# Rows of three chunks turned by transposing transfers on the SyncE queue in place of TensorE transposes, with later loads issued behind the normalising

## The chip, the cores and the metric

The kernel runs on one core of one Trainium2 chip. A core has five engines that run side by side, each through its own list of instructions in a fixed order: TensorE (PE in the profile; PEld is its weight load), VectorE (DVE), ScalarE (ACT), GpSimd (POOL) and SyncE (SP), which here does nothing but issue DMA transfers. Engines wait for one another by semaphores. On-chip memory has 128 partitions; matrix results land in a separate memory, PSUM. The metric is the device time of one execution in microseconds (us): 178.88 us as the median of three runs of the kernel before (178.66 to 179.46).

## The reference

The input is a matrix of 2048 rows (tokens) by 512 columns. Each row is normalised, and two branches work on the normalised rows: a two-dimensional Fourier filter and a gated feed-forward layer of width 1792. The result is the sum of the input and both branches, in bf16.

```python
def _A_ref(x, w_r, w_i):                    # x: 1 x 2048 x 512
    X = rfft2(x.astype(float32))            # 2048 x 257
    X = X * (w_r + 1j * w_i)
    return irfft2(X, s=(S, D)).astype(bfloat16)

def _B_ref(x, w_gate, w_up, w_down):        # 512 x 1792, 512 x 1792, 1792 x 512
    g = einsum("bsd,df->bsf", x, w_gate)
    u = einsum("bsd,df->bsf", x, w_up)
    return einsum("bsf,fd->bsd", gelu(g) * u, w_down)

x = A_x
xn = _layernorm(x, axis=-1)
return x + _A_ref(xn, A_w_r, A_w_i) + _B_ref(xn, B_w_gate, B_w_up, B_w_down)
```

## The kernel before

**Tiling.** The 2048 rows are 16 row tiles of 128 rows (s = 0 to 15), in four chunks of four tiles (b = 0 to 3). `x_sb` holds the rows, `specB` among other things the normalised rows (`xn`, L500: eight buffers, tile s uses buffer s mod 8), and `xnT` the normalised rows turned, that is, with the 512 columns on the partitions in four blocks of 128. Everything that TensorE does with the rows reads `xnT`.

**A row tile's way.** `stats` (L503) takes mean and variance on DVE, `root_pool` (L513) the reciprocal root on POOL for four tiles at once, `norm` (L519) writes the normalised tile on DVE. `turn` (L524) turns one or two tiles: four PE transposes of 128 by 128 per tile into a PSUM buffer, and one DVE copy from there to `xnT` (L539). Tiles 0 to 3 are turned one by one, tiles 4 to 15 in pairs.

**The feed-forward branch.** `gated` (L648) multiplies a chunk with one block of 128 columns of `w_gate` and of `w_up` (PE, L657), ACT brings both results from PSUM to `gg` and `uu` (four buffers each, L662 and L663), DVE multiplies them into `hT` (L664). `down` (L692) multiplies `hT` with `w_down` (`wd`). The list `filler` (L722 on) gives the order of this work: chunk 0, then chunk 1 with the down products of chunk 0 among it, and so on; the down products of chunk 3 end the kernel.

**The spectral branch.** `fold` (L545) adds and subtracts parts of a turned chunk on DVE and multiplies it on PE with `smallc` (L570). After four chunks DVE does butterflies, PE multiplies with `tokf` (L782), DVE multiplies with the filter `filt` (L450, between L795 and L843), PE multiplies with `toki` (L859, L860), DVE does butterflies again, PE multiplies with `smallc` (L924), and the result is added to `x_sb`. `filt` holds the filter twice: as it is, and mirrored. The mirrored half is made by six transfers from the inputs to a scratch tensor in device memory, `w_mirror` (L616 to L618), and loaded from there. POOL computes two small tensors, `edge`, one from the real and one from the imaginary part of the whole filter (L792).

**What sets the order.** All instructions are operations of a planner (`_Sched`). Each has a planned cost, a key or a due time, and its predecessors follow from what it reads and writes. The planner steps through time, and of the operations that an engine can start next it takes the one with the lowest priority number: the time at which it becomes ready plus its key, or its due time. The order of each engine is then fixed in the program; at run time an instruction waits for its semaphores and everything behind it on its engine waits too. For a transfer the planner counts a cost on the issuing queue and then a common pipe for all bytes; the costs are written in the code, 0.41 us for a plain transfer, and 3.5, 2.5 and 2.0 us for the three mirror transfers of each part.

**Transfers on SP.** In order: rows and weights of the feed-forward branch, `smallc`, the rows of chunks 2 and 3, then `wd`, `tokf`, `toki` (L608 to L610), the six mirror transfers, the direct and mirrored loads of `filt`, and a few small ones. All of these have no predecessor but the first row tile's load (the list `gate`, whose entries every later transfer on SP takes as predecessors, L445), the mirrored loads excepted, which follow the mirror transfers. The result's stores come last.

Of the kernel before, what the change touches and what calls it, by code (L numbers as in the profile page):

```python
# [16 lines left out]
NFC = 14  # L17
# [111 lines left out]
class _Sched:  # L129
# [11 lines left out]
    def op(self, eng, cost, fn, reads=(), writes=(), tiles=(), key=0.0, after=(), dma=0, lag=0.0, due=None):  # L141
        o = _Op()
        o.eng, o.fn, o.cost, o.key, o.dma, o.lag, o.due = eng, fn, cost, key, dma, lag, due
        o.reads, o.writes, o.tiles = reads, writes, [(t, False) for t in tiles]
        o.extra = [a for a in after if a is not None]
        o.seq = len(self.ops)
        o.end = None
        o.pos = None
        self.ops.append(o)
        return o  # L150
# [182 lines left out]
def bass_parallel_sum__spectral_gfnet__glu_gated_geglu__prompt_kernel(  # L333
# [19 lines left out]
    wdv = B_w_down.rearrange("(fc p) d -> p fc d", p=P)  # L353

    sch = _Sched()
    op = sch.op

    with ExitStack() as es:
        def sb(name, shape, dt=BF16, cell=0):
            n = int(np.prod(shape))  # L360
            t = es.enter_context(nc.sbuf_tensor(name, [P, n], dt))
            return view(t, name, 0, shape, cell)
# [14 lines left out]
        xnT = sb("xnT", [4, 4, 4, P])  # L377
        wg = sb("wg", [4, FF])
        wu = sb("wu", [4, FF])
        wd = sb("wd", [NFC, D])  # L380
# [61 lines left out]
        gate = []  # L442

        def dma(q, dst, src, nbytes, wr=None, rd=None, key=0.0, after=(), cost=0.41, lag=0.0):
            after = tuple(after) + tuple(gate if q == "sp" else ())  # L445
            return op(q, cost, lambda e: e.dma_start(dst() if callable(dst) else dst.ap, src() if callable(src) else src.ap),  # L446
                      reads=rd if rd is not None else (), writes=wr if wr is not None else (), dma=nbytes, key=key, after=after, lag=lag)
# [7 lines left out]
        def load(q, dst, src, nbytes, **kw):  # L455
            return dma(q, dst, lambda: src, nbytes, wr=(dst,), **kw)

        def blk(s):
            return (s - 1) % 16
# [4 lines left out]
        k = iter(np.arange(0.0, 1.0, 0.001))  # L464
        first_row = None
        for s in range(4):
            o = load("sp", x[:, s], xb[:, blk(s), :], 131072, key=next(k))
# [32 lines left out]
        def xn(s):  # L500
            return RB(8192 + 512 * (s % 8), [4, P])

        def stats(s, key, due=None, after=()):  # L503
            op("dve", 0.61, lambda e: e.bn_stats(bst[:, s].ap, xs(s).ap), reads=(xs(s),), writes=(bst[:, s],), key=key, due=due, after=after)  # L504
            op("dve", 0.11, lambda e: e.bn_aggr(bag[:, s].ap, bst[:, s].ap), reads=(bst[:, s],), writes=(bag[:, s],), key=key, due=due)
# [7 lines left out]
        def root_pool(s0, n, key):  # L513
            sl = slice(s0, s0 + n)
            v, y, h = vv[:, sl], rs[:, sl], half[:, sl]
            op("pool", 0.2 + 0.03 * n, lambda e: e.tensor_scalar(v.ap, bag.ap[:, sl, 1], LN_EPS, None, ADD), reads=(bag[:, sl],), writes=(v,), key=key)
            op("pool", 0.5 + 0.14 * n, lambda e: e.tensor_tensor(y.ap, v.ap, h.ap, ALU.pow), reads=(v, h), writes=(y,), key=key)

        def norm(s, key, due=None):  # L519
            o, i = xn(s).rs([512]), xs(s)  # L520
            op("dve", 0.34, lambda e: e.tensor_scalar(o.ap, i.ap, bag.ap[:, s, 0:1], rs.ap[:, s:s + 1], SUB, MUL),
               reads=(i, bag[:, s], rs[:, s:s + 1]), writes=(o,), key=key, due=due)

        def turn(s0, n, key):  # L524
            b, sl = s0 // 4, s0 % 4
            t = _T("sp")

            def bank():
                return ps_sp_bf[:, t.slot * 2048:t.slot * 2048 + 512 * n]

            def f(e):
                ins = None
                for i in range(4 * n):
                    ins = e.transpose(bank()[:, i * P:(i + 1) * P], xn(s0 + i // 4).ap[:, i % 4], ident.ap)  # L534
                return ins

            o = xnT[:, b, sl:sl + n].rs([512 * n])
            op("pe", 4 * n * 0.056, f, reads=tuple(xn(s0 + i) for i in range(n)) + (ident,), tiles=(t,), key=-40, lag=0.1)
            op("dve", 0.08 + n * 0.26, lambda e: e.tensor_copy(o.ap, bank()), writes=(o,), tiles=(t,), key=key)  # L539


        Y = R1(0, [8, 2, D])
        H = R3(0, [8, 2, D])
        X = R1(0, [8, 2, D])
        def fold(b):  # L545
            par = b % 2
            a = RB(2048 * par, [4, 2, P])
            f = RB(4096 + 2048 * par, [4, 4, P])
            z = R3(2048 * par, [2, 2, 512])
            xt = xnT[:, b]  # L550
            kk = 2.0
            tt(a, xt[:, :, 0:2], xt[:, :, 2:4], ADD, 1024, kk)
            tt(f[:, :, 0], a[:, :, 0], a[:, :, 1], ADD, 512, kk)
            tt(f[:, :, 1], a[:, :, 0], a[:, :, 1], SUB, 512, kk)
            tt(f[:, :, 2:4], xt[:, :, 0:2], xt[:, :, 2:4], SUB, 1024, kk)
            fv = f.rs([2, 2, 4, P])
            zv = z.rs([2, 2, 4, P])
            tt(zv[:, :, 0], fv[:, :, 1], fv[:, :, 0, :, ::-1], ADD, 1024, kk)
            tt(zv[:, :, 1], fv[:, :, 1], fv[:, :, 0, :, ::-1], SUB, 1024, kk)
            for j in range(2):  # L560
                t = _T("sp")

                def f_c(e, z=z, j=j, t=t):
                    ins = None
                    for o in range(2):
                        bank = spb(t, o).rearrange("p (s r i) -> p s r i", s=2, r=4)
                        for cc in range(4):
                            to = bank[:, :, 2 * cc] if cc < 2 else bank[:, :, 1::2]
                            mat = Tf.ap[:, cc] if cc < 2 else Tf.ap[:, 2 * cc - 2:2 * cc]
                            ins = e.matmul(to, z.ap[:, j, o, cc * P:(cc + 1) * P], mat, start=(cc == 0), stop=(cc == 3))  # L570
                    return ins

                op("pe", 4 * 0.057 + 4 * 0.11, f_c, reads=(z[:, j], Tf), tiles=(t,), key=kk, lag=0.1)
                jp = 2 * b + j
                yv = Y[:, jp].rs([4, 64, 4])
                op("act", c_act(1024), lambda e, yv=yv, t=t: e.activation(yv.ap, spair(t).rearrange("p (s r i) -> p s i r", s=4, r=4), ACT.Copy),  # L576
                   writes=(yv,), tiles=(t,), key=-0.5)
# [18 lines left out]
        for s in range(4, 16):  # L596
            stats(s, 0.0, STAT[0] + STAT[1] * (s - 4))
            if s % 4 == 3:
                root_pool(s - 3, 4, -4.0)
        for s in range(4, 16):  # L600
            norm(s, 0.0, NORM[0] + NORM[1] * (s - 4))
            if s % 2 == 1:
                turn(s - 1, 2, 1.0)
            if s % 4 == 3:
                fold(s // 4)


        load("sp", wd, wdv, NFC * 131072, key=next(k))  # L608
        load("sp", tf, c_tf.ap().rearrange("p (t v m) -> p t v m", t=3, v=8), 786432, key=next(k))
        load("sp", ti, c_ti.ap().rearrange("p (v t q) -> p v t q", v=8, t=3), 786432, key=next(k))  # L610
        scr, far, near = {}, {}, {}
        for ri, src in ((0, A_w_r), (1, A_w_i)):
# [178 lines left out]
        for ri, f in ((0, ADD), (1, SUB)):  # L791
            op("pool", 0.3, lambda e, ri=ri, f=f: e.tensor_tensor(edge.ap[:, ri], ev[0].ap[:, ri], ev[1].ap[:, ri], f),  # L792
               reads=(ev[0][:, ri], ev[1][:, ri]), writes=(edge[:, ri],), key=1.0)
# [53 lines left out]
        for v in range(8):  # L847
            t = _T("sp")

            def f_i(e, v=v, t=t):  # L850
# [15 lines left out]
               writes=(gv,), tiles=(t,), key=-0.5)  # L866
# [109 lines left out]
```

## Time and profile before

| | |
|---|---|
| median of 3 runs | 178.88 us (178.66 to 179.46) |
| the profiled execution | 178.78 us |
| its span (first to last instruction) | 177.0 us |
| TensorE clock granted | 1.00 in every stretch |
| PE / DVE / ACT / POOL busy | 97% / 78% / 60% / 6% of the span |
| PE busy, 10.5 to 162 us | all of it |
| transfers | 14.97 MB, most of it in the first 29 us |

Times in the profile are microseconds from the start of the span. A group's line gives the line of the code, engine, operation, what is written and read, shapes and count, then busy time and the mean of one in ns, then the idle time of its engine ahead of it and what ended it. A line of a timeline gives start, duration and the same names, with `[idle <-releaser]` where the engine had stood still; several alike in a row are one line. SPq marks the issuing of a transfer by SP, not its landing. The chain of waits goes back from the last instruction, at each step to what released it or to the instruction before it on its engine.

### The profile page before, as it was taken

Reading aid. Unit: us, or ns where it says so; the run is one execution under the profiler, and the core shown is the slowest. Engines: PE = TensorE matmul, PEld = TensorE weight load, DVE = VectorE, ACT = ScalarE, POOL = GpSimd, SP = SyncE. Lnnn points to the kernel's source line nnn. Section 1 sums busy time; section 2 is a strip of 40 time slices with the busy share of each in tenths; the row PEclk is TensorE's granted clock in tenths of the full one; section 3 lists DMA queues with packets and bytes.
Section 4 is the critical chain, followed back from the end, with each engine's and each line's share of the span. In section 5 each row is a group of like instructions: output and inputs, shape, how many; then the busy total and the mean of one; then the engine's idle time right before and its main releaser. Section 6 shows DMA issues by size and latency. Waiting matters only on the chain.

```text
span 177.0 us, 2757 instructions
## 1 busy us (share of the span) xinstructions
PE 172.4 (97%) x1052; PEld 90.8 (51%) x1052; DVE 137.8 (78%) x270; ACT 106.4 (60%) x172; POOL 10.1 (6%) x19
## 2 busy tenths in 40 slices
PE   7889999999999999999999999999999999999994
PEld 2678665456554444444544644445664444444443
DVE  3869899999969939999999799999599812121931
ACT  3478775658685798363894966363995636362000
POOL 2120420300000230000000000000000000000000
DMA  5999997222363710000000000000004200000311
GB/s 167 335 351 356 349 371 266 61 65 47 66 151 87 176 38 4 0 0 0 0 6 0 0 0 0 0 4 0 0 19 132 91 0 0 0 4 0 119 59 61
DMA packets 17773, 14.97 MB, mean 85 GB/s; under 512 B 1119, under 2 KB 17376, under 8 KB 17760
## 3 DMA queue, kind: packets, MB, share of 16 engines
q1 hardware_dynamic: 16560, 13.94, 26.3%
q10 hardware_dynamic: 1200, 0.85, 1.6%
q8 instruction: 8, 0.13, 0.3%
q14 instruction: 5, 0.04, 0.1%
HBM read 12.70 MB, written 3.15 MB: 90 GB/s over the span
## 4 chain that ended last, share of the span: by engine, by line
PE 93%; DMA 5%; SPq 1%; issue 0%; DVE 0%
PE ps_gu L657 53%; PE ps_dn L702 20%; PE ps_sp L702 7%; PE ps_sp L782 3%; DMA wu<-in_B_w_up_dram 3%; PE ps_sp L570 3%; PE ps_sp L924 2%; PE ps_sp L534 2%; DMA x_sb<-in_A_x_dram 1%; PE ps_sp L859 1%; PE ps_sp L860 1%; SPq L446 1%; DVE x_sb L713 0%
## 5 line engine op out<-in xcount | busy, mean ns | idle before, releaser
L657 PE MATMUL ps_gu<-xnT,wu 128*128 128x512 bf16 (+1 forms) x236 | 56.7, 363 | 0.6 <-DMA wu<-in_B_w_up_dram 0.6
L657 PE MATMUL ps_gu<-xnT,wg 128*128 128x512 bf16 (+1 forms) x236 | 56.7, 363 | 0.0
L663 ACT ACTIVATE uu<-ps_gu 128x512 bf16<-128x512 f32 (+1 forms) x59 | 33.9, 574 | 13.2 <-PE ps_gu L657 12.9
L662 ACT ACTIVATE gg<-ps_gu 128x512 bf16<-128x512 f32 (+1 forms) x59 | 34.0, 576 | 12.2 <-PE ps_gu L657 11.6
L702 PE MATMUL ps_dn<-wd,hT 128*128 128x512 bf16 x168 | 38.5, 379 | 0.0
L657 PEld LDWEIGHTS ps_gu<-xnT,wu 128*128 128x128 bf16 x236 | 22.7, 98 | 22.9 <-ACT uu L688 0.8
L657 PEld LDWEIGHTS ps_gu<-xnT,wg 128*128 128x128 bf16 x236 | 22.6, 98 | 21.5 <-DVE xnT L539 0.3
L664 DVE TENSOR_TENSOR hT<-gg,uu 128x512 bf16<-128x512 bf16 (+1 forms) x59 | 22.7, 394 | 11.6 <-ACT uu L663 11.5
L702 PEld LDWEIGHTS ps_dn<-wd,hT 128*128 128x128 bf16 x168 | 16.4, 98 | 19.4
L450 DVE TENSOR_TENSOR specB<-specB 128x1024 bf16<-128x1024 bf16 (+2 forms) x37 | 23.5, 669 | 2.1 <-ACT specB L929 2.0
L710 ACT ACTIVATE db<-ps_dn 128x512 bf16<-128x512 f32 x12 | 7.2, 597 | 23.4 <-PE ps_dn L702 23.4
L504 DVE BATCH_NORM_STATS2 bst<-x_sb 128x6 f32<-128x512 bf16 x16 | 10.9, 685 | 3.7 <-DMA x_sb<-in_A_x_dram 3.5
L450 DVE TENSOR_TENSOR specB<-specA 128x2048 bf16<-128x2048 bf16 x8 | 9.4, 1220 | 4.0 <-ACT specA L787 2.1
L702 PE MATMUL ps_sp<-wd,hT 128*128 128x512 bf16 (+2 forms) x70 | 12.3, 336 | 0.0
L711 DVE TENSOR_TENSOR x_sb<-db,x_sb 128x512 bf16<-128x512 bf16 x12 | 5.0, 418 | 7.8 <-ACT db L710 7.8
L450 DVE TENSOR_TENSOR specC<-specB 128x1024 bf16<-128x1024 bf16 (+1 forms) x14 | 10.0, 759 | 0.0
L702 PEld LDWEIGHTS ps_sp<-wd,hT 128*128 128x128 bf16 x70 | 6.4, 98 | 6.1 <-DVE x_sb L713 0.2
L450 DVE TENSOR_TENSOR specB<-specB,filt 128x2048 bf16<-128x2048 bf16 x8 | 9.4, 1215 | 0.0
L787 ACT ACTIVATE specA<-ps_sp 128x1024 bf16<-128x1024 f32 x8 | 7.9, 1027 | 2.0 <-PE ps_sp L782 1.9
L929 ACT ACTIVATE specB<-ps_sp 128x1024 bf16<-128x1024 f32 x8 | 8.5, 1090 | 0.0
L576 ACT ACTIVATE specA<-ps_sp 128x1024 bf16<-128x1024 f32 x8 | 7.8, 1021 | 0.3
L865 ACT ACTIVATE specC<-ps_sp 128x1024 bf16<-128x1024 f32 x8 | 7.8, 1042 | 0.0
(63 smaller groups left out, 141.2 us busy)
## 6 DMA issues: line engine op xcount, KB each, us to landing
out_dram<-x_sb SPq DMA_DIRECT2D x15, 128.0 KB, 1.8
wd<-in_B_w_down_dram SPq DMA_DIRECT2D x1, 1792.0 KB, 13.3
x_sb<-in_A_x_dram SPq DMA_DIRECT2D x3, 512.0 KB, 8.4
wg<-in_B_w_gate_dram SPq DMA_DIRECT2D x2, 512.0 KB, 8.4
wu<-in_B_w_up_dram SPq DMA_DIRECT2D x2, 512.0 KB, 8.7
filt<-w_mirror SPq DMA_DIRECT2D x6, 128.5 KB, 2.3
tokf<-c_tf SPq DMA_DIRECT2D x1, 768.0 KB, 13.7
toki<-c_ti SPq DMA_DIRECT2D x1, 768.0 KB, 9.7
```

Of the source, the lines that this page charges most:

```text
L450: return op("dve", c_tt(n), lambda e: e.tensor_tensor(o.ap, a.ap, b.ap, f), reads=(a, b), writes=(o,), key=key, **kw)
L504: op("dve", 0.61, lambda e: e.bn_stats(bst[:, s].ap, xs(s).ap), reads=(xs(s),), writes=(bst[:, s],), key=key, due=due, after=after)
L576: op("act", c_act(1024), lambda e, yv=yv, t=t: e.activation(yv.ap, spair(t).rearrange("p (s r i) -> p s i r", s=4, r=4), ACT.Copy), writes ...
L657: ins = e.matmul(gub(t, n), w.ap[:, dc, fc * P:(fc + 1) * P], xnT.ap[:, b, sl, dc, :], start=(dc == 0), stop=(dc == 3))
L662: op("act", c_act(n), lambda e: e.activation(gg.ap[:, gs.slot, 0:n], gub(g, n), ACT.Gelu_apprx_tanh), tiles=(g, gs), key=0.0)
L663: op("act", c_act(n), lambda e: e.activation(uu.ap[:, us.slot, 0:n], gub(u, n), ACT.Copy), tiles=(u, us), key=0.0)
L664: op("dve", c_tt(n), lambda e: e.tensor_tensor(hT.ap[:, h.slot, lo:lo + n], gg.ap[:, gs.slot, 0:n], uu.ap[:, us.slot, 0:n], MUL), tiles=(g ...
L702: ins = e.matmul(bank(), hT.ap[:, hs[(b, fc)].slot, sl * P:(sl + 1) * P], wd.ap[:, fc, lo:lo + n], start=(fc == 0), stop=(fc == NFC - 1))
L710: op("act", c_act(n), lambda e: e.activation(db.ap[:, d.slot, 0:n], bank(), ACT.Copy), tiles=(t, d), key=0.0)
L787: op("act", c_act(1024), lambda e, xv=xv, t=t: e.activation(xv.ap, spair(t), ACT.Copy), writes=(xv,), tiles=(t,), key=-0.5)
L865: op("act", c_act(1024), lambda e, gv=gv, t=t: e.activation(gv.ap, spair(t).rearrange("p (k x i) -> p k x i", k=4, x=4), ACT.Copy), writes ...
L929: op("act", c_act(1024), lambda e, rv=rv, t=t: e.activation(rv.ap, spair(t), ACT.Copy), writes=(rv,), tiles=(t,), key=-0.5)
```

## The change

Tiles 4 to 15 are no longer turned by PE and copied by DVE. A new operation on SP, `turn_dma`, issues one transfer per tile that reads the 128 by 512 normalised tile and writes it turned into `xnT`; the planner charges it 1.25 us on the queue and 262144 bytes of pipe, with key -5. `hold[s]` is the norm operation of tile s. `wd` is issued only after tile 7 is normalised; `tokf` and every transfer on SP that follows it in the code only after tile 11; `toki` and all that follows only after tile 15 (the mirror transfers, all loads of `filt` and of `filt1024`). The turning of tiles 0 to 3 stays as it was.

```diff
+        def turn_dma(s):
+            i, o = xn(s), xnT[:, s // 4, s % 4]
+            op("sp", 1.25, lambda e: e.dma_start_transpose(o.ap, i.rs([512]).ap), reads=(i,), writes=(o,), dma=262144, key=-5.0)
+
...
+        hold = {}
         for s in range(4, 16):
             norm(s, 0.0, NORM[0] + NORM[1] * (s - 4))
-            if s % 2 == 1:
-                turn(s - 1, 2, 1.0)
+            hold[s] = sch.ops[-1]
+            turn_dma(s)
             if s % 4 == 3:
                 fold(s // 4)
 
 
-        load("sp", wd, wdv, NFC * 131072, key=next(k))
+        load("sp", wd, wdv, NFC * 131072, key=next(k), after=(hold[7],))
+        gate.append(hold[11])
         load("sp", tf, c_tf.ap().rearrange("p (t v m) -> p t v m", t=3, v=8), 786432, key=next(k))
+        gate.append(hold[15])
         load("sp", ti, c_ti.ap().rearrange("p (v t q) -> p v t q", v=8, t=3), 786432, key=next(k))
```

## The prediction

> **What bounds the kernel now.** I read the busy table, then the chain of waits, then the engines' timelines around the lines that the diff touches, last the list of waits.
>
> ```profile
> PE 172.4 (97%) x1052; PEld 90.8 (51%) x1052; DVE 137.8 (78%) x270; ACT 106.4 (60%) x172; POOL 10.1 (6%) x19
> ...
> PE 93%; DMA 5%; SPq 1%; issue 0%; DVE 0%
> ```
>
> PE works 97% of the span and carries 93% of the chain that ended last. In the chain told in order of time, PE is never released by anything else after 10.49 us. So a microsecond of PE work removed is a microsecond gained, and a microsecond in which PE stands still is one lost, since its order is fixed when the program is built. What the edit takes from PE and DVE, by form (count | busy us, mean ns | idle before) and in the chain (start us, us):
>
> ```profile
> L534 PE MATMUL ps_sp<-smallc,specB 128*128 128x128 bf16 x64 | 4.7, 219 | 0.0
> L539 DVE COPY xnT<-ps_sp 128x1024 bf16<-128x1024 bf16 x6 | 4.0, 672 | 0.0
> ...
> 29.55 0.89 PE ps_sp L534 x16
> 38.21 0.89 PE ps_sp L534 x16
> ```
>
> And the SP queue, which takes the new work (start us, us of issuing):
>
> ```profile
> 13.94 1.42 SPq L446 DMA_DIRECT2D wd<-in_B_w_down_dram  x1
> 15.40 5.80 SPq L446 DMA_DIRECT2D tokf<-c_tf  x1
> 21.24 0.43 SPq L446 DMA_DIRECT2D toki<-c_ti  x1
> 21.72 11.69 SPq L446 DMA_DIRECT2D w_mirror<-in_A_w_r_dram  x3
> 33.45 10.17 SPq L446 DMA_DIRECT2D w_mirror<-in_A_w_i_dram  x3
> 43.66 5.71 SPq L446 DMA_DIRECT2D filt<-in_A_w_r_dram  x6
> ...
> 57.21 4.41 SPq L446 DMA_DIRECT2D filt<-w_mirror  x9
> ```
>
> From toki on SP issues without a break for 40 us. The filter is complete only at the end of that, and this is where it is used:
>
> ```profile
> 60.87 2.29 POOL L792 TENSOR_TENSOR edge<-filt 128x16 bf16<-128x16 bf16 x1 [25.61 <-DMA filt<-w_mirror]
> 63.36 0.22 POOL L792 TENSOR_TENSOR edge<-filt 128x16 bf16<-128x16 bf16 x1 [0.20 <-DMA filt<-w_mirror]
> ...
> 68.94 0.26 DVE L826 TENSOR_TENSOR edge<-specA,edge 128x16 bf16<-128x16 bf16 x2
> 69.12 4.63 DVE L450 TENSOR_TENSOR specB<-specB,filt 128x2048 bf16<-128x2048 bf16 x4
> ...
> 86.12 0.22 PE L859 MATMUL ps_sp<-toki,specA 128*128 128x128 bf16 x1
> ```
>
> POOL starts the moment the real half of the filter has landed (60.87) and again when the imaginary half has (63.36). DVE needs them at 68.94, so the filter has 5.6 us to spare today. Whatever moves SP's chain from 21.24 on by more than that arrives in DVE's queue.
>
> **PE's part.** 48 of the 64 transposes go. In the chain 16 of them advance PE by 0.89 us: 3 x 0.89 = 2.67 us off PE, all before 39.1 us. DVE sheds the six copies of 128x1024, 4.0 us, all before 41.6 us.
>
> **SP's part, the new order.** Norms of tiles 4 to 7 run at 21.15, of 8 to 11 at 27.20, of 12 to 15 at 35.55 (four in 1.36 to 1.38 us, timeline of DVE). A turn is the planner's first choice (key -5) as soon as its tile is normalised; wd waits for tile 7, tokf for tile 11, and toki with all mirror and filter transfers for tile 15, behind four more turns.
>
> What SP spends on issuing one turn no row shows. Bounds: 0.43 us, the plain 128 KB-class issue (the toki row), and 3.9 us, the mean of the first three mirror transfers (11.69/3), the costliest kind there is. Nearest in shape are the loads of 512 rows (x_sb, wg, wu), which take from 0.51 us (at 5.16) to 1.3 us (at 12.1) as the queue fills. I take 1.25, near the upper of these, which is also what the diff charges.
>
> Then: turns 4 to 7 from 21.55 (first norm done) to 26.55; wd 1.42, to 28.0; tiles 8 to 11 are ready by then; four turns to 33.0; tokf 0.5, to 33.5. Tiles 12 to 15: I let their norms come 1.5 to 2 us earlier than 35.55, because four of the six copies (2.7 us of DVE) no longer stand ahead of them; the first is done at 34.0. Four turns to 39.0. **toki goes out at 39.0 instead of 21.24, 17.8 us later.**
>
> Costed at nothing, with their cover: chunk 1, turned by 26.6 plus some 2.3 us of landing (as the small filter loads take), is wanted by PE at 35.46, less 1.78 for transposes gone: 4.8 us of cover. wd, issued at 26.6, is wanted at 45.90 and took 13.3 us to land in a full queue: 3 us or more. tokf is wanted at 56.93, toki at 86.12. Chunks 2 and 3 are wanted by folds on DVE about when the copies end today (33.6 and 41.6); the last turn lands near 41.3. If a turn costs 2 us or more this cover is gone too.
>
> **From toki to the whole filter.** Now 60.87 - 21.24 = 39.6 us for the real half and 63.36 - 21.24 = 42.1 us for the imaginary one. Some of it is queueing behind the bulk loads: in the view of the DMA rates the rate falls from over 400 GB/s to 149 only at 29.0, 7.7 us after toki's issue, and the first three mirror issues take 11.69 against 10.17 for the second three. So the chain shortens by 1.5 to 7.7 us; I take the middle, 4.6. Real half at 39.0 + 35.0 = 74.0, imaginary half at 39.0 + 37.5 = **76.5 us**.
>
> **What then waits.** The four products with the filter (4.63 us, 1.16 each) stand in DVE's fixed order. As it is now the two small edge products go first and need both halves: POOL 0.22, the edges 0.26, the products 4.63, done at 81.6 instead of 73.75, 7.85 us late. Should the planner put the two with the real half first, they fit before 76.5 and the end is 78.8, 5.1 late. I take the middle, 6.5. Behind them on DVE stand the gating products (the next one today at 73.67). Until these run, gg and uu (four slots each) stay full, ACT stops emptying PSUM, and PE, with two gated pairs already held when DVE stops, gets through two more and then fills its three banks: it stands. Once the products are done DVE works on at its pace (today 11.2 us to the last edge write at 84.95), and PE's L859 starts 1.0 us after that need (its weights at 85.9). So L859 comes 6.5 - 1.0 = **5.5 us late**, at 91.6, and what PE does from there to the end is what it does today. The 2.67 us saved earlier lie ahead of this wait and are swallowed by it.
>
> **A cold PE.** After the wait PE may start slowly: the ten warming matmuls at the start are 0.43 us apart, the 512-column ones later 0.216, so 4.3 us of the slow pace cost 2.1 us. Whether a pause in mid-run brings it back no row shows, since PE makes none. Between 0 and 2.1 I take 1.0. The Trainium skill, TensorE: Matmul & The Clock Gate, under "Why this matters for your kernels", warns of gaps of more than about 3 us between bursts of matmuls; by it the whole 2.1 us would be due and the sum 186.4.
>
> **Sum.** Profiled execution 178.78 us (span 177.0 and 1.8 around it; the runs' median 178.88, a tenth above). 178.78 + 5.5 + 1.0 = **185.3 us**.
>
> **Rival 1, the filter comes in time (not slower).** Place: the filter products; decisive point: filter complete by about 68.9, or the planner puts them so much later among the fill work that nothing waits. PE has work that needs no spectral result to spare (131.5 to 162.57). Then only PE's saving shows: 178.8 - 2.7 = 176.1. Against it: the chain would have to be 30 us long instead of 42, while the second three mirror issues, beside no bulk load, still took 10.17. And the planner's own charges for six mirror transfers sum to 16 us where SP shows 21.9, so it counts on the filter too early and will not leave the room. With both favourable bounds (0.43 per turn, so toki at 35.6; chain shorter by 7.7) the imaginary half is there at 70.0 and the products end between 72.3 and 75.1, within 1.4 us of today on either side: with the 1.0 us of slack, 176.4 to 179.1. Chance 0.12 for this and what lies between.
>
> **Rival 2, a turn is much dearer.** Above 1.25 us SP has no gap left between 21.55 and toki, so each further microsecond counts twelve times. At 2.5 us: toki at 21.55 + 30 + 1.9 = 53.5, 14.5 later than assumed, time 200. At 3.9: toki at 70, 31 later, time 216, and chunk 1 itself (37.2 plus landing) is late for PE. For it: the transposing transfer moves its tile in small pieces, and the rows with small pieces, mirrors and filter loads, are the slow ones. Against: none of the loads of 128 partitions took SP over 1.9 us except behind a full queue. Chance 0.18.
> The Trainium skill, VectorE: DVE Perf Modes, under "The three transpose paths", gives 1309 ns for a 128x128 block through the DMA crossbar; by an estimate from that page, four blocks a tile and one after another, twelve tiles are 63 us and this rival would be its worst end. Its Advanced Engine Details and Errata, under "X-Bar Transpose (TRN2)", calls such transfers as fast as plain ones, which is my forecast's case; no row here decides.
>
> **How the numbers follow.** Forecast 0.70, rival 1 0.12, rival 2 0.18. The forecast's own range: at 0.43 per turn toki goes out at 35.6, 3.4 earlier than assumed, time 181.9; at 2.0 at 47.5, 8.5 later, time 193.8; the two orders of the products add 1.4 either way. The range that leaves a tenth on each side runs from 180.5 to 198. About 0.5% is what a measurement of this kernel can tell from no change; faster by more 0.09, within it 0.04, slower 0.87.
>
> **What would show it.** Right: toki issued near 39; POOL's edge operations released by the filter near 74 to 80; DVE idle ahead of the filter products, put down to POOL or to the filter's transfer; PE idle some 6 us in all between 75 and 95, none elsewhere; 16 matmuls at L534. Wrong in size: another issue time of the turns. Wrong altogether: POOL's edge operations released before 69, PE never idle after 10.5; or PE idle already before 45, waiting for xnT or wd.

## The result, and the profile after

The changed kernel takes 184.79 us (median of 4 runs, 183.97 to 185.06) against 178.95 for the kernel before: a ratio of 1.0315, 95% interval 1.0273 to 1.0357. It is slower by 5.8 us. The profiled execution has a span of 182.2 us, 5.2 more than before. In the changed kernel the lines from the normalising on are shifted: the turn is L543, gated products L664 (before L657), ACT's two reads of them L669 and L670, gating products on DVE L671, down products L709 (L702), the edges L799 on POOL and L833 on DVE (L792, L826), the products with `toki` L866 (L859).

First the SP queue in time (start us, us of issuing):

```profile
22.10 5.23 SPq L543 DMA_TRANSPOSE xnT<-specB  x4
27.38 0.58 SPq L446 DMA_DIRECT2D wd<-in_B_w_down_dram  x1
28.00 8.45 SPq L543 DMA_TRANSPOSE xnT<-specB  x4
36.49 0.58 SPq L446 DMA_DIRECT2D tokf<-c_tf  x1
37.12 5.13 SPq L543 DMA_TRANSPOSE xnT<-specB  x4
42.29 0.58 SPq L446 DMA_DIRECT2D toki<-c_ti  x1
42.91 7.55 SPq L446 DMA_DIRECT2D w_mirror<-in_A_w_r_dram  x3
50.51 9.67 SPq L446 DMA_DIRECT2D w_mirror<-in_A_w_i_dram  x3
```

From 22.1 on the queue has no gap. toki, and behind it everything that belongs to the filter, is issued at 42.29 instead of 21.24. Next POOL and DVE, in time, where the filter is used:

```profile
79.26 0.22 POOL L799 TENSOR_TENSOR edge<-filt 128x16 bf16<-128x16 bf16 x1 [45.20 <-DMA filt<-w_mirror]
80.30 0.62 POOL L799 TENSOR_TENSOR edge<-filt 128x16 bf16<-128x16 bf16 x1 [0.81 <-DMA filt<-w_mirror]
```

```profile
68.58 2.36 DVE L450 TENSOR_TENSOR specB<-specA 128x2048 bf16<-128x2048 bf16 x2 [2.69 <-ACT specA L794]
79.52 0.18 DVE L833 TENSOR_TENSOR edge<-specA,edge 128x16 bf16<-128x16 bf16 x1 [8.59 <-POOL edge L799]
```

The filter's halves are there at 79.3 and 80.3 (before: 60.9 and 63.4). DVE finishes the step ahead of the products at 70.9 and then stands for 8.6 us, with the gating products queued behind. The list of waits (waiter, whom for: us in all, times, longest) shows how that comes to PE:

```profile
DVE edge L833 <- POOL edge L799: 8.6, 1, 8.6
ACT gg L669 <- DVE hT L671: 7.7, 2, 3.9
...
PE ps_gu L664 <- ACT gg L669: 5.1, 2, 2.6
...
DVE specB L450 <- DMA xnT<-specB: 3.3, 2, 2.0
...
PE ps_sp L574 <- DVE specC L450: 0.8, 1, 0.8
```

DVE's wait holds hT, hT holds gg, gg holds PE. The last two lines are a second, smaller loss: the folds of chunks 2 and 3 wait for their turned rows, and PE for a fold. PE in time:

```profile
85.79 1.04 PE L664 MATMUL ps_gu<-xnT,wu 128*128 128x512 bf16 x4 [2.60 <-ACT gg L669]
86.66 1.54 PE L664 MATMUL ps_gu<-xnT,wg 128*128 128x512 bf16 x4
90.67 1.89 PE L664 MATMUL ps_gu<-xnT,wu 128*128 128x512 bf16 x4 [2.46 <-ACT gg L669]
92.35 1.78 PE L664 MATMUL ps_gu<-xnT,wg 128*128 128x512 bf16 x4
93.96 1.03 PE L664 MATMUL ps_gu<-xnT,wu 128*128 128x512 bf16 x4
...
96.34 0.22 PE L866 MATMUL ps_sp<-toki,specA 128*128 128x128 bf16 x1
```

Four such matmuls take 1.03 us at the usual pace; from the second group after the first pause on they take 1.54 to 1.89, until 94. The table by stretch says the same (stretch, its length, busy us of PE, PEld, DVE, ACT, POOL with their instructions, granted clock, DMA share, GB/s):

```profile
34.00:46.00 12.00, 11.16 (x72) 6.20 (x71) 8.65 (x21) 8.51 (x12) 0.06 (x1) 1.00 1.19 226
...
75.00:95.00 20.00, 14.94 (x59) 5.96 (x58) 15.48 (x22) 6.87 (x12) 0.85 (x2) 0.83 0.11 26
```

PE stands 0.84 us in the first of these, 5.06 in the second, at a mean clock of 0.83. Against before that makes -2.67 (transposes) + 0.84 + 5.06 = 3.2 of the 5.2 us. The other 2.0 fit the slow pace, which can be read off above: the three groups of 1.54, 1.89 and 1.78 us take 2.1 us more than three of 1.03. The balance holds to about half a microsecond; the kernel before, for one, also stood 0.56 us for `wu` at 10.49, which the changed one did not.

### The profile page after: what moved, and what is told of

The parts are those of the page before. It is cut to its first block, busy times and chain, and to the rows that moved or that the text cites. A ratio compares the mean times of both kernels' runs of the same rounds, so it can differ in the third digit from the quotient of the medians.

```text
span 182.2 us, 2677 instructions
## 1 busy us (share of the span) xinstructions
PE 172.2 (95%) x1004; PEld 88.5 (49%) x1004; DVE 134.4 (74%) x264; ACT 106.6 (59%) x172; POOL 9.0 (5%) x19
## 2 busy tenths in 40 slices
DMA packets 24301, 16.54 MB, mean 91 GB/s; under 512 B 7647, under 2 KB 23904, under 8 KB 24288
## 4 chain that ended last, share of the span: by engine, by line
PE 49%; SPq 20%; DVE 13%; DMA 11%; issue 5%; ACT 0%; POOL 0%; DVEq 0%; POOLq 0%; ACTq 0%
PE ps_gu L664 25%; SPq L446 20%; PE ps_dn L709 13%; PE ps_sp L709 7%; DMA x_sb<-in_A_x_dram 7%; DVE specB L450 6%; DVE bst L504 3%; DMA xnT<-specB 2%; PE ps_sp L931 2%; DVE hT L671 2%; DMA filt<-in_A_w_r_dram 1%; DVE specB L521 1%; PE ps_sp L866 1%; PE ps_sp L867 1%; DVE specC L450 1%
## 5 line engine op out<-in xcount | busy, mean ns | idle before, releaser
L664 PE MATMUL ps_gu<-xnT,wu 128*128 128x512 bf16 (+1 forms) x236 | 57.6, 367 | 5.1 <-ACT gg L669 5.1
L664 PE MATMUL ps_gu<-xnT,wg 128*128 128x512 bf16 (+1 forms) x236 | 58.0, 369 | 0.0
L669 ACT ACTIVATE gg<-ps_gu 128x512 bf16<-128x512 f32 (+1 forms) x59 | 33.5, 568 | 19.8 <-PE ps_gu L664 11.4
L670 ACT ACTIVATE uu<-ps_gu 128x512 bf16<-128x512 f32 (+1 forms) x59 | 33.7, 570 | 11.8 <-PE ps_gu L664 11.4
L709 PE MATMUL ps_dn<-wd,hT 128*128 128x512 bf16 x168 | 38.9, 379 | 0.0
L664 PEld LDWEIGHTS ps_gu<-xnT,wu 128*128 128x128 bf16 x236 | 22.9, 99 | 30.1 <-ACT gg L669 6.5
L664 PEld LDWEIGHTS ps_gu<-xnT,wg 128*128 128x128 bf16 x236 | 23.0, 99 | 23.1 <-issue 1.0
L671 DVE TENSOR_TENSOR hT<-gg,uu 128x512 bf16<-128x512 bf16 (+1 forms) x59 | 22.5, 393 | 10.7 <-ACT uu L670 10.7
L709 PEld LDWEIGHTS ps_dn<-wd,hT 128*128 128x128 bf16 x168 | 16.3, 98 | 18.9
L504 DVE BATCH_NORM_STATS2 bst<-x_sb 128x6 f32<-128x512 bf16 x16 | 10.9, 685 | 4.1 <-DMA x_sb<-in_A_x_dram 4.0
L709 PE MATMUL ps_sp<-wd,hT 128*128 128x512 bf16 (+2 forms) x70 | 12.3, 336 | 0.0
L709 PEld LDWEIGHTS ps_sp<-wd,hT 128*128 128x128 bf16 x70 | 6.4, 98 | 6.1 <-DVE x_sb L720 0.2
L936 ACT ACTIVATE specB<-ps_sp 128x1024 bf16<-128x1024 f32 x8 | 7.8, 1031 | 0.3 <-PE ps_sp L931 0.3
```

The source lines that it names most:

```text
L664: ins = e.matmul(gub(t, n), w.ap[:, dc, fc * P:(fc + 1) * P], xnT.ap[:, b, sl, dc, :], start=(dc == 0), stop=(dc == 3))
L669: op("act", c_act(n), lambda e: e.activation(gg.ap[:, gs.slot, 0:n], gub(g, n), ACT.Gelu_apprx_tanh), tiles=(g, gs), key=0.0)
L670: op("act", c_act(n), lambda e: e.activation(uu.ap[:, us.slot, 0:n], gub(u, n), ACT.Copy), tiles=(u, us), key=0.0)
L671: op("dve", c_tt(n), lambda e: e.tensor_tensor(hT.ap[:, h.slot, lo:lo + n], gg.ap[:, gs.slot, 0:n], uu.ap[:, us.slot, 0:n], MUL), tiles=(g ...
L709: ins = e.matmul(bank(), hT.ap[:, hs[(b, fc)].slot, sl * P:(sl + 1) * P], wd.ap[:, fc, lo:lo + n], start=(fc == 0), stop=(fc == NFC - 1))
L936: op("act", c_act(1024), lambda e, rv=rv, t=t: e.activation(rv.ap, spair(t), ACT.Copy), writes=(rv,), tiles=(t,), key=-0.5)
```

## The experiments

Two theories were set against each other. A: the loss is the filter, which is complete some nine microseconds after DVE, in its fixed order, wants it. B: the loss is in the turning transfers themselves, late folds and a crowded queue.

**The filter earlier, the turns as they are.** The six mirror transfers are left out and the mirrored half is loaded straight from the inputs.

```diff
-            scr[ri] = nc.dram_tensor("w_mirror%d" % ri, (9, P, 257), BF16, kind="Internal").ap()
-            far[ri] = [
...
-            load("sp", W[:, ri, 1, 1], scr[ri][0], 65792, after=(far[ri][0],), key=1.0 + next(k))
+            load("sp", W[:, ri, 1, 1], r16[:, 12], 65792, key=1.0 + next(k))
...
-                load("sp", W[:, ri, 1, 2 * c:2 * c + 2], scr[ri][4 - c::4][0:2].rearrange("c m k -> m c k"), 131584, after=tuple(far[ri]), key=1.0 + next(k))
+                load("sp", W[:, ri, 1, 2 * c:2 * c + 2], r16[:, 4 + c:4 + c + 9:8], 131584, key=1.0 + next(k))
```

> The changed kernel without the six mirror transfers: the mirrored half of the filter is loaded straight from the inputs, unmirrored rows in place of the mirrored ones, so that part of the filter has other values. The turns, their places in SP's queue and what waits for them stay. Theory A (the loss is the filter that comes after DVE's products were due): toki still goes out near 42, the 31 filter loads take about 18.4 us behind it, so the filter is complete near 63 to 64, before DVE reaches the products near 71; PE stands only for the 0.84 us ahead of the folds near 41.5; time 178.8 - 2.7 + 0.8 = 176.9 us. Rival B (the loss is in the turning transfers themselves, late folds and a crowded queue): these are as before, time stays at 183 us or more.

Measured: 177.02 us, ratio to the kernel before 0.9888 (0.9846 to 0.9931). The turns are unchanged (5.23, 8.49 and 5.12 us of issuing), toki goes out at 42.34, and in POOL's timeline the filter is there at 62:

```profile
62.07 2.48 POOL L796 TENSOR_TENSOR edge<-filt 128x16 bf16<-128x16 bf16 x2 [27.99 <-DMA filt<-in_A_w_r_dram]
```

DVE reaches the products with the filter at 70.96 and waits for none of it. In PE's timeline the only pause after the first 11 us is that ahead of a fold:

```profile
42.27 1.49 PE L574 MATMUL ps_sp<-smallc,specC 128*128 128x128 bf16 x16 [0.38 <-DVE specC L450]
```

> The kernel before with the same part left out: no mirror transfers, the mirrored half of the filter loaded from the inputs unmirrored. The control to the run above. In the kernel before the filter has 5.6 us to spare, so both theories expect no change: 178.9 us, within 0.5%.

Measured: 179.26 us, ratio 1.0001 (0.9977 to 1.0025). So the transfers left out were worth nothing in the kernel before and some 7.6 us in the changed one (ratios of 1.0315 and 0.9888). B falls: with all twelve turns in place the kernel is 1.1% faster than before. The planner makes its order anew for each kernel, so this run alone does not part the filter's time from the order; the runs below do. And what the turns take from SP's queue, so that toki is issued later, belongs to A.

**The later loads alone.** The kernel before with the three holds and no turning transfer (e_hold_only in what follows).

```diff
+            hold[s] = sch.ops[-1]
...
-        load("sp", wd, wdv, NFC * 131072, key=next(k))
+        load("sp", wd, wdv, NFC * 131072, key=next(k), after=(hold[7],))
+        gate.append(hold[11])
...
+        gate.append(hold[15])
```

> The kernel before, PE turning all tiles, with only the later issue of the loads: wd behind the norm of tile 7, tokf behind tile 11, toki and all mirror and filter transfers behind tile 15. Theory A: tile 15 is normalised near 36.9, toki goes out near 37 (42.3 in the changed kernel), the filter is complete near 37 + 38 = 75, five to six us after the 69 to 70 at which the products stand in DVE's order; PE stands for about that less its 1 us of slack; time 182 to 184 us, slower than before without a single turning transfer. Rival B: 178.9 us, no change, as no turning transfer is issued.

Measured: 183.19 us, ratio 1.0222 (1.0173 to 1.0271). The timelines of SP, of POOL (when the second half of the filter is there) and of PE:

```profile
37.13 0.34 SPq L446 DMA_DIRECT2D toki<-c_ti  x1
```

```profile
75.01 1.23 POOL L796 TENSOR_TENSOR edge<-filt 128x16 bf16<-128x16 bf16 x1 [1.35 <-DMA filt<-w_mirror]
```

```profile
89.81 0.23 PE L863 MATMUL ps_sp<-toki,specA 128*128 128x128 bf16 x1 [2.75 <-DVE specA L830]
```

Moving the loads is the larger part of the loss: 4.0 us without one turn. The products with `toki` start at 89.81 instead of 86.12, 3.7 us late, and that is the kernel's loss. The turns push toki from 37.1 to 42.3 on top of it and give PE 2.7 us back.

**The planner told.** The changed kernel with every transfer as it is; only the costs change by which the planner places the work (e_told in what follows). On SP that moves one turn: five stand between `wd` and `tokf` instead of four.

```diff
-            op("sp", 1.25, lambda e: e.dma_start_transpose(o.ap, i.rs([512]).ap), reads=(i,), writes=(o,), dma=262144, key=-5.0)
+            op("sp", 1.6, lambda e: e.dma_start_transpose(o.ap, i.rs([512]).ap), reads=(i,), writes=(o,), dma=262144, key=-5.0)
...
-        def dma(q, dst, src, nbytes, wr=None, rd=None, key=0.0, after=(), cost=0.41, lag=0.0):
+        def dma(q, dst, src, nbytes, wr=None, rd=None, key=0.0, after=(), cost=0.6, lag=0.0):
...
-                dma("sp", lambda ri=ri: scr[ri][0:4], lambda c16=c16: c16[12:16, ::-1, :], 526336, key=next(k), cost=3.5, lag=6.0),
-                dma("sp", lambda ri=ri: scr[ri][5:8], lambda c16=c16: c16[5:8, ::-1, :], 394752, key=next(k), cost=2.5, lag=6.0)]
-            near[ri] = dma("sp", lambda ri=ri: scr[ri][4:9:4, 0:64], lambda c16=c16: c16[0:9:8, 127:63:-1, :], 131584, key=next(k), cost=2.0, lag=5.0)
+                dma("sp", lambda ri=ri: scr[ri][0:4], lambda c16=c16: c16[12:16, ::-1, :], 526336, key=next(k), cost=1.4, lag=14.0),
+                dma("sp", lambda ri=ri: scr[ri][5:8], lambda c16=c16: c16[5:8, ::-1, :], 394752, key=next(k), cost=3.4, lag=14.0)]
+            near[ri] = dma("sp", lambda ri=ri: scr[ri][4:9:4, 0:64], lambda c16=c16: c16[0:9:8, 127:63:-1, :], 131584, key=next(k), cost=3.75, lag=14.0)
```

> The changed kernel with other planner costs on SP alone, near what its profile shows: 1.6 us for a turn, 0.6 for a plain load, 1.4, 3.4 and 3.75 for the three mirror transfers of each part with a lag of 14. Every transfer is the same and toki still goes out near 42 to 43, the filter is complete near 80, but the orders of DVE and PE are made for that. Theory A: PE has fill work to do until then, the products stand later in DVE's order, and what is left is PE's saving: 176 to 177 us, faster than both kernels. Rival B: the turning transfers cost what they cost, 183 us or more.

Measured: 176.66 us, ratio 0.9866 (0.9827 to 0.9906), faster than both kernels. The filter comes no earlier than in the changed kernel; POOL's and DVE's timelines show what fills the time:

```profile
80.83 2.44 POOL L799 TENSOR_TENSOR edge<-filt 128x16 bf16<-128x16 bf16 x2 [47.11 <-DMA filt<-w_mirror]
```

```profile
73.66 0.42 DVE L671 TENSOR_TENSOR hT<-gg,uu 128x512 bf16<-128x512 bf16 x1 [1.79 <-ACT uu L670]
75.39 0.42 DVE L671 TENSOR_TENSOR hT<-gg,uu 128x512 bf16<-128x512 bf16 x1 [1.30 <-ACT uu L670]
77.11 0.42 DVE L671 TENSOR_TENSOR hT<-gg,uu 128x512 bf16<-128x512 bf16 x1 [1.30 <-ACT uu L670]
78.84 0.42 DVE L671 TENSOR_TENSOR hT<-gg,uu 128x512 bf16<-128x512 bf16 x1 [1.30 <-ACT uu L670]
80.79 2.40 DVE L450 TENSOR_TENSOR specB<-specB,filt 128x2048 bf16<-128x2048 bf16 x2 [1.52 <-DMA filt<-w_mirror]
```

The gating products now stand ahead of the filter products. DVE still waits, for 1.5 us, but nobody waits for DVE: PE is busy from 75 to 95 without a pause. Two controls belong to it, the same costs in kernels without turns.

> The kernel before with the planner costs of e_told for loads and mirror transfers (0.6; 1.4, 3.4 and 3.75 with a lag of 14). The control to e_told: if the costs alone made a faster order, the kernel before would gain too. Theory A: PE never waited for the filter there, so 179 us, no change within 0.5%. A rival to A (the costs improve the order as such): 177 us or less.

Measured: 179.78 us, ratio 1.0020 (0.9986 to 1.0053). The costs alone bring nothing.

> e_hold_only (PE turns all tiles, loads issued later) with the same planner costs. Theory A: toki still goes out near 37 and the filter is complete near 75, but the products are ordered for it: the 4 us that e_hold_only lost come back, 179 us, and the distance from here to e_told, some 2.5 us, is PE's 48 transposes. Rival (late loads cost time by themselves, whatever the order): 182 to 184 us as e_hold_only.

Measured: 179.02 us, ratio 1.0015 (0.9981 to 1.0049). The 4 us that the later loads cost are gone, although the filter is complete at 74.9 as it was (75.0). From here to the turning kernel with the same costs it is 2.4 us by the medians and 2.7 by the ratios (1.0015 and 0.9866, each to the kernel before timed beside it); the 48 transposes are 2.67 us of PE.

**What makes a turn slow.** In the changed kernel the second group of turns takes 8.45 us to issue, the others 5.2. The next kernel is that of "The planner told" (e_told), with wd and tokf issued only after all turns (the edit is against e_told):

```diff
-        load("sp", wd, wdv, NFC * 131072, key=next(k), after=(hold[7],))
-        gate.append(hold[11])
+        gate.append(hold[15])
+        load("sp", wd, wdv, NFC * 131072, key=next(k), after=(hold[15],))
...
-        gate.append(hold[15])
```

> e_told with wd and tokf, too, held behind the normalising of tile 15, so that no bulk load stands in the queue while tiles 8 to 15 are turned. If a turn is dear to issue because a bulk load drains in front of it (turns 8 to 11 took 8.45 us behind wd, 4 to 7 took 5.23), all twelve take 1.3 us each, 15 to 16 us, and land in 2.5 us; if it is the number of turns under way, tiles 8 to 11 stay at 2 us each. wd then lands near 46, when PE wants its first down product; time 176.5 to 178 us.

Measured: 178.68 us, ratio 0.9984 (0.9948 to 1.0020). By tile, the turns of the changed kernel (ns of issuing, min/median/max; us to landing), and then those of this one:

```profile
L543 SPq DMA_TRANSPOSE xnT<-specB x12: 1203/1265/2554, 22.1 to 41.0; - x12
...
DMA to landing us min/median/max: 2.5/4.2/9.1
```

```profile
L543 SPq DMA_TRANSPOSE xnT<-specB x12: 1188/1264/2010, 21.7 to 37.4; - x12
...
DMA to landing us min/median/max: 2.4/2.5/4.1
```

It was wd: without a bulk load in front a turn lands in 2.5 us (median), and eleven of the twelve take 1.19 to 1.31 us to issue; one took 2.01, and why is open. All twelve are out in 16.95 us, a wait of 0.6 us for tile 8 included. The smaller bulk load, `tokf` of 768 KB, had not made the issue dear: in the changed kernel the four turns behind it took 1.20 to 1.27 us each, though 3.0 to 5.5 us to land. The time was missed by little, 178.7 where at most 178 was expected. The bulk loads now stand ahead of the mirror transfers, whose first three take 13.24 us to issue instead of 7.55 (8.04 in e_told), and the filter is complete only at 84.8, later than the order was made for: DVE waits 5.3 us for it and PE 2.7 us.

**The turns without the holds.**

```diff
-        load("sp", wd, wdv, NFC * 131072, key=next(k), after=(hold[7],))
-        gate.append(hold[11])
+        load("sp", wd, wdv, NFC * 131072, key=next(k))
...
-        gate.append(hold[15])
```

> The changed kernel without the three holds: turns on SP, but the loads keep their early place, so a turn comes behind wd, tokf, toki, the mirror transfers and the direct filter loads that the planner lists first. The SP queue is then free for turns only near 55; chunk 1 is turned near 62, where PE wants it near 34. PE stands for about 28 us; time 200 to 210 us. If the holds were what makes the changed kernel slow and the turns could do without, it would be under 180 us.

Measured: 199.11 us, ratio 1.1120 (1.1033 to 1.1207), just under the stated range. SP's timeline and PE's waits:

```profile
53.14 13.08 SPq L543 DMA_TRANSPOSE xnT<-specB  x10
```

```profile
PE ps_gu L662 <- DMA xnT<-specB: 15.4, 1, 15.4
```

The first turn goes out at 53 and PE stands 15.4 us for chunk 1, not 28: the planner had put three down products of chunk 0 (L707, from 33.5 on) ahead of it. Another 3.1 us go ahead of a fold at 73.28. So behind these loads the turns come too late, and the holds, as shown, cost time unless the planner knows of the delay.

## Why the prediction was right, point by point

- **The bound and the place: right.** PE stood for the filter, through DVE, hT and gg as described, and the experiment that brings the filter earlier takes all of the loss away.
- **PE's saving: right in size.** Where nothing waits, 2.4 to 2.7 of the 2.67 us appear. The prediction let the wait swallow them in the changed kernel; no run tests that, but it is likely, as PE with its transposes would have come later to its pauses and stood less.
- **PE does from there to the end what it does today: wrong, by 5.0 us.** From the first product with `toki` to the end PE needs 182.2 - 96.34 = 85.9 us; before it was 177.0 - 86.12 = 90.9. The planner, presumably because it counts with the holds and with its own cost of the turns, put 23 more matmuls of 512 columns ahead of that product (16 gated, 7 down; 0.216 us each, 5.0 us).
- **How much PE stands: the sum and its own sign did not fit.** A product with `toki` 5.5 us late, with 2.67 us less work ahead of it, means 8.2 us of standing still, where the prediction listed some 6. Measured are 5.9 (5.06 and 0.84). With 5.0 us more work, 2.1 of slow pace and the 2.67 gone that makes 10.3; the product came 10.2 us late.
- **One turn on SP: 1.25 us assumed, 1.27 measured in a free queue.** Mis-sized were the four behind wd: 5.0 us assumed, 8.45 measured. With a start 0.55 us later, and wd out in 0.58 instead of 1.42, toki went out at 42.3 instead of 39.0. (The lower bound was misread: the toki row with its 0.43 us is a transfer of 768 KB, not of the 128 KB class.) Rival 2 stayed away: all twelve took 18.8 us of SP's time.
- **From toki to the filter: right.** 35.0 and 37.5 us assumed, 37.0 and 38.0 measured, against 39.6 and 42.1 before.
- **How late the products are: mis-sized.** Assumed 6.5 us, with their end at 78.8 to 81.6; their last one ended at 84.6, 10.9 us late. 3.3 us of it is toki's issue. The first half of the filter came 37.0 us after toki, 2.0 later than assumed, and the products could not start before it. PE's product with `toki` came 10.2 us late; 5.5 of waiting and 1.0 of a cold PE were assumed.
- **A cold PE: mis-sized, at its upper bound.** 1.0 us assumed between 0 and 2.1; the groups at the slow pace lost 2.1.
- **Costed at nothing:** chunk 1, wd, tokf and toki were in time. The folds of chunks 2 and 3 were not: DVE waited 2.0 and 1.4 us for their rows, and the first of these cost PE 0.84 us before 45, which the prediction had listed as a sign of being wrong. It is a seventh of PE's standing; the rest is where it was forecast.

So 185.3 us was close to 184.79 (the profiled execution took 183.97) with the right mechanism, but in part by luck: the product with `toki` came 3.7 us later than the 6.5 assumed, and 5.0 us less work followed it.

## What to carry to other kernels

A transfer that is moved behind others on a queue carries its whole chain with it; measure from its issue to the last use, and compare with the spare time at that use, which here was 5.6 us for a move of 21. Where an order is fixed in advance, lateness that the planner knows of costs nothing while there is other work, and lateness that it does not know of is paid for once the spare time and the work queued ahead are used up: give it the durations that a profile shows, and look again after each change of the queue. A transfer that is cheap to issue in a free queue had another price behind the bulk load of 1.8 MB on the same queue.

## What was not expected of the hardware

A turning transfer of a 128 by 512 tile moves many small packets: the count under 512 B rises from 1119 to 7647, that is 544 per turn. Beside nothing else it is issued in 1.27 us and lands in 2.5; behind a 1.8 MB load it took up to 2.55 us to issue and up to 9.1 to land.

The slow pace of PE came back after short pauses in one kernel and not in another. In the changed kernel it set in near 87.1, in the second group of matmuls after a pause of 2.60 us, and lasted over a second pause of 2.46 us until 94; the granted clock from 87 to 94 is 0.51, and the row of granted clock in the profile shows it (40 slices of 4.6 us):

```profile
PEclk9999999999999999999569999999999999999999
```

In the kernel with the later loads alone a pause of 2.75 us ahead of L863, ten microseconds after one of 0.63, cost no pace in the profiled execution: the clock of that stretch stayed at 1.00. Another execution of the same kernel had a mean clock of 0.991 where the rest had 0.999 or 1.00; where its slow spell lay no record shows. In the kernel without the holds the clock fell with the pause of 15.4 us and again around that of 3.06 (0.83 from 70 to 80). The Trainium skill, TensorE: Matmul & The Clock Gate, under "Why this matters for your kernels", warns of gaps of more than about 3 us; the changed kernel shows the slow pace after a shorter one. Whether the moment at which the pause falls makes the difference was not tried; the second pause does not, as the slow pace had set in before it.
